# Attention and feed-forward on one core: v pieces as two transfers, early q and k turned in four quadrants, sums shared with GpSimd, and a new order

## The chip, the cores and the metric

The kernel runs on one core of a Trainium2 chip. The time is that of one execution on the device, in microseconds (us), and the median of several runs is compared. The core has five instruction streams: TensorE (PE, with its weight loads shown as PEld), VectorE (DVE), ScalarE (ACT), GpSimd (POOL) and SyncE (SP). SP issues every DMA of this kernel, one after the other, from one queue.

## The reference

```python
def _attn_ref(q, k, v):                 # 8 batches, 8 heads, 576 tokens, 64 per head
    q_d = q.reshape(B, H, Sd, factor, D).mean(axis=3)     # factor 4, Sd = 144; k_d and v_d alike
    out_d = sm_attn(q_d, k_d, v_d)                        # softmax attention over pooled tokens
    out_up = np.repeat(out_d, factor, axis=2)
    mask = np.abs(pos[:, None] - pos[None, :]) < factor   # local attention, 3 tokens each way
    ...
    return out_up + out_local

def _moe_ref(x, w_in, w_out, g_ln):     # x: 4608 tokens of 512, from all heads
    h = x @ w_in                        # 512 -> 1024
    sm = softmax(h)
    solu = h * sm
    ln = (solu - mean) / sqrt(var + 1e-06) * g_ln
    return ln @ w_out                   # 1024 -> 512
```

The weights come in as 64-bit floats and are turned into pairs of 32-bit values on the chip.

## The kernel before

**Tiles and stages.** Each of the 8 batches has 4 pairs of heads. Its q and k are brought into a layout with the head dimension on the partitions (tiles `qT`, `kT`), summed in groups of four tokens (`qd_flat`, `kd`, function `sums`), and used twice: class `Pooled` computes the pooled attention in two halves g (tiles `sd` for scores, `pd` for weights, `pdt`/`pdT` for their transposes, `po` for the output), and the classes `Local` and `PairOfLocals` the local attention in windows (tiles `sc`, `pl`, `plt`/`plT`, `xp`). Both add into `x`, one tile for each batch. `x` is cut into 36 tiles of 128 tokens for the feed-forward part: `xhl` splits such a tile into `xh` and `xl`, `ffn_in` multiplies by the first weights (`h`, line 813) and computes `e` and its statistics, `u` goes through DRAM to be transposed (`v<-u`), and `ffn_out` multiplies by the second weights (`o`, line 934). Four of the 36 span two batches; a tile needs all additions into the x of its batches.

**The early batches.** Batches 0 and 1 (`EARLY = 2`) are prepared by `EarlyBatch`: `load_one` brings one pair of q or k with plain rows, and `pair_steps` turns it on PE by small matmuls with the identity, 18 for q and then 18 for k, each kind in two quadrants of 64x64, followed by a copy out of PSUM. The later batches use many DMAs with short runs (line 257) and DVE's transposes (lines 445 and 449).

**The v pieces.** The pooled attention needs v summed by four tokens. `load_vs` brings one of three pieces `vs` of a batch: partitions 0 to 63 hold heads 0 to 3 and partitions 64 to 111 heads 4 to 7, for 48 groups of four tokens. For an early batch it issues four transfers (line 294), one for each pair of heads h and h + 4, each with a source of 2 heads x 64 rows x 1 KB. For a later batch it issues two (line 297), one of 64 partitions and one of 48, each with 4 heads x 1 KB for a partition. `pooled_vsum` (lines 466 and 469) adds each piece up into `vd`, which the `po` matmuls (line 795) read.

**The weights.** 16 pieces of 512 KB are loaded at the start (line 337); each takes four DVE operations (lines 348 to 361), of which one can go to GpSimd, and one subtraction.

**What sets the order.** The kernel makes a list of about 1800 steps (`plan`) and issues them in the order of the table `ORDER`, word for word; no scheduler moves anything afterwards. For steps in the table `OTHER`, `engine(usual, instead)` takes the second engine. So each engine's instructions, and SP's DMAs, stand in one fixed order, and an instruction that waits holds everything behind it on its engine. Buffers come from pools (six of `big` for the v pieces and weights, five of `vw` for the v windows of the local attention); a DMA into a buffer waits until its last reader is done.

**PE's idle time.** 24 steps (`keep_clock`, line 991) issue two matmuls each that compute nothing (`warm`), placed where PE would otherwise wait.

## Time and profile before

| | us |
|---|---|
| median of 3 runs | 638.21 (638.14 to 639.31) |
| the profiled execution | 636.78 |
| its span, first to last instruction | 635.0 |
| PE busy in the span | 569.0 (90%) |
| DVE, ACT, POOL busy | 455.6, 339.0, 282.8 |
| moved by DMA | 101.67 MB, 160 GB/s on average |

The span starts at the first instruction; places in it are given in us from there. A row of the chain of waits or of the timeline gives the start, the length, the engine, the line of the kernel, and the tile that is written, `<-`, the tiles that are read. SPq is time of SP's queue in issuing a DMA; a DMA row is the time from its issue until it landed. A row of the groups gives the busy time in all and the mean of one in ns, then the engine's idle time just before them and what ended it.

### The profile page before, as it was taken

What the parts mean: (1) busy time and instruction counts of PE and PEld (TensorE: products, weight loads), DVE (VectorE), ACT (ScalarE), POOL (GpSimd) and SP (SyncE); (2) the same over time, 40 slices, a digit from 0 to 9 for tenths busy, and PEclk for the clock granted to TensorE, in tenths of its full rate; (3) what the DMA queues carried; (4) which work ended last, traced back from release to release, by engine and by line L of the source; (5) the groups of instructions that cost most, each with busy time, mean ns of one, the idle gap of its engine ahead of it and who ended that gap; (6) DMA issues with size and microseconds to landing.
All of it is one profiled execution on the core that took longest, in us unless ns stands there. A gap on an engine that the chain in (4) does not pass through costs nothing.

```text
span 635.0 us, 17193 instructions
## 1 busy us (share of the span) xinstructions
PE 569.0 (90%) x6940; PEld 447.6 (70%) x6940; DVE 455.6 (72%) x673; ACT 339.0 (53%) x702; POOL 282.8 (45%) x365
## 2 busy tenths in 40 slices
PE   7863689951999999998999799899999999999997
PEld 4552567740777777777777677778887878778775
DVE  5953589942898977976986898477878688665451
ACT  4634567822468546754465447455653646453352
POOL 2540557821455945434284335724345444322211
PEclk9986789985899989999999899899999999999999
DMA  8344748723889868779786666755876384432341
GB/s 312 103 157 113 201 142 176 168 81 97 177 202 198 200 175 212 175 176 211 197 169 171 169 192 177 151 154 139 186 194 183 102 194 150 118 101 86 112 134 50
DMA packets 208255, 101.67 MB, mean 160 GB/s; under 512 B 163376, under 2 KB 192432, under 8 KB 208176
## 3 DMA queue, kind: packets, MB, share of 16 engines
q1 hardware_dynamic: 208176, 100.58, 60.6%
q8 instruction: 54, 0.88, 0.6%
q14 instruction: 25, 0.20, 0.1%
HBM read 67.51 MB, written 27.79 MB: 150 GB/s over the span
## 4 chain that ended last, share of the span: by engine, by line
PE 56%; SPq 15%; DMA 11%; DVE 9%; issue 3%; POOL 3%; ACT 3%; DVEq 0%; ACTq 0%; POOLq 0%
PE o L934 24%; PE h L813 20%; DMA vs<-in_v_dram 5%; SPq L257 4%; SPq L294 4%; SPq L886 2%; SPq L276 2%; PE po L795 2%; PE xp L696 2%; PE warm L991 2%; DMA v<-u 2%; PE sd L734 1%; PE pdt L776 1%; DMA qm<-in_q_dram 1%; SPq L270 1%
## 5 line engine op out<-in xcount | busy, mean ns | idle before, releaser
L934 PE MATMUL o<-wo_h,uh 128*128 128x512 f32 x288 | 119.2, 414 | 1.8 <-ACT osb L941 1.8
L813 PE MATMUL h<-wi_h,xh 128*128 128x512 f32 x288 | 116.4, 404 | 1.2 <-DVE e L827 1.2
L934 PE MATMUL o<-wo_l,uh 128*128 128x512 f32 x288 | 115.8, 402 | 0.0
L813 PE MATMUL h<-wi_l,xh 128*128 128x512 f32 x288 | 114.5, 398 | 0.0
L813 PE MATMUL h<-wi_h,xl 128*128 128x512 f32 x288 | 114.2, 397 | 0.0
L917 POOL TENSOR_TENSOR ul<-v,uh 128x512 fp32r<-128x512 f32 x39 | 51.5, 1321 | 79.1 <-ACT uh L914 67.7
L934 PE MATMUL o<-wo_h,ul 128*128 128x512 f32 x288 | 79.5, 398 | 0.9 <-DVE ul L917 0.8
L825 ACT ACTIVATE e<-h,st 128x1024 f32<-128x1024 f32 x36 | 40.1, 1115 | 63.7 <-DVE st L822 60.2
L934 PEld LDWEIGHTS o<-wo_h,uh 128*128 128x128 f32 x288 | 55.4, 192 | 17.5 <-ACT osb L941 2.6
L822 DVE TENSOR_REDUCE st<-h 128x1 f32<-128x1024 f32 x36 | 43.7, 1215 | 32.3 <-PE h L813 30.4
L907 DVE STREAM_TRANSPOSE v<-v 128x512 f32<-128x512 f32 x70 | 47.1, 691 | 27.2 <-DMA v<-u 27.2
L813 PEld LDWEIGHTS h<-wi_h,xh 128*128 128x128 f32 x288 | 54.5, 189 | 15.7 <-issue 1.4
L934 PEld LDWEIGHTS o<-wo_h,ul 128*128 128x128 f32 x288 | 54.1, 189 | 15.3 <-DVE ul L917 1.5
L813 PEld LDWEIGHTS h<-wi_h,xl 128*128 128x128 f32 x288 | 54.5, 189 | 14.0 <-DVE xl L968 0.7
L934 PEld LDWEIGHTS o<-wo_l,uh 128*128 128x128 f32 x288 | 55.4, 192 | 12.0
L813 PEld LDWEIGHTS h<-wi_l,xh 128*128 128x128 f32 x288 | 54.6, 189 | 12.3
L914 ACT ACTIVATE uh<-v 128x512 fp32r<-128x512 f32 x70 | 43.5, 624 | 34.6 <-DVE v L907 17.1
L831 POOL TENSOR_SCALAR st<-st 128x1 f32<-128x1 f32 x36 | 11.9, 331 | 101.0 <-DVE e L827 100.7
L827 DVE SCALAR_TENSOR_TENSOR e<-h,e 128x1024 f32<-128x1024 f32 x36 | 43.6, 1211 | 13.9 <-ACT e L825 13.6
L865 ACT ACTIVATE e<-e 128x1024 f32<-128x1024 f32 x35 | 36.8, 1052 | 17.2 <-DMA u<-e 17.2
L941 ACT ACTIVATE osb<-o,s 128x512 f32<-128x512 f32 x36 | 24.5, 680 | 36.1 <-PE o L934 15.1
L853 ACT ACTIVATE e<-e,st 128x1024 f32<-128x1024 f32 x27 | 30.9, 1145 | 14.1 <-POOL st L831 12.4
(124 smaller groups left out, 1087.1 us busy)
## 6 DMA issues: line engine op xcount, KB each, us to landing
u<-e SPq DMA_DIRECT2D x35, 512.0 KB
v<-u SPq DMA_DIRECT2D x140, 128.0 KB
out_dram<-osb SPq DMA_DIRECT2D x36, 256.0 KB
qm<-in_q_dram SPq DMA_DIRECT2D x96, 72.0 KB
km<-in_k_dram SPq DMA_DIRECT2D x96, 72.0 KB
vw<-in_v_dram SPq DMA_DIRECT2D x80, 64.0 KB
vw<-in_v_dram SPq DMA_DIRECT2D x40, 128.0 KB
plT<-pl SPq DMA_DIRECT2D x80, 64.0 KB
```

Source lines behind the costliest of these rows:

```text
L257: nc.sync.dma_start(t[nm][Q * 32:Q * 32 + 32, pr], src[b, 2 * pr + par, :, dh * 32:dh * 32 + 32].rearrange("(k t) d -> t k d", t=32),)
L294: nc.sync.dma_start(vs[:, h], source(h, [[H // 2 * S * D, 2], [FAC * D, 64]]))
L813: nc.tensor.matmul(hps[:, n, :], src[:, cc, :], wt[:, cc, n * 512:(n + 1) * 512], start=(cc == 0 and src is xh and wt is wi_h), stop=(cc = ...
L822: nc.vector.tensor_reduce(out=nmx, in_=hf, op=ALU.max, axis=AX.X, negate=True)
L825: nc.scalar.activation(e, hf, AF.Exp, bias=nmx, scale=1.0, accum_out=se)
L827: nc.vector.scalar_tensor_tensor(out=e, in0=hf, scalar=1.0, in1=e, op0=ALU.mult, op1=ALU.mult, accum_out=su)
L853: nc.scalar.activation(e, e, AF.Identity, bias=nmu, scale=1.0)
L865: nc.scalar.activation(e0, e, AF.Square, accum_out=m2)
L907: nc.vector.transpose(vg, vg)
L914: nc.scalar.activation(uh, tp, AF.Copy)
L917: (usual if v is None else engine(usual, nc.vector)).tensor_tensor(out=ul, in0=tp, in1=uh.bitcast(F32), op=ALU.subtract)
L934: nc.tensor.matmul(o, src[:, j, :], wt[:, 4 * g + j, :], start=(g == 0 and j == 0 and src is uh and wt is wo_h), stop=(g == 1 and j == 3 a ...
```

## The change

- `load_vs` uses for all batches the two transfers of 64 and 48 partitions that the later batches had.
- `EarlyBatch.pair_steps` turns q and k of a pair in one step, their 36 matmuls alternating; k is stored one head lower (`load_one` loads heads 2p+1 and 2p+2 together, and heads 0 and 7 alone), so that q uses two quadrants of PE and k the other two. The k tiles always come from the pool `ps_h`.
- `sums` may go to GpSimd, as three additions in place of one reduction.
- The pooled output that is not a batch's first is copied from PSUM into a part of the `pd` tile, and added into `x` from there, on GpSimd or on DVE.
- `ORDER` and `OTHER` are new tables: all steps are put in a new order, and OTHER has 157 entries in place of 103.

In the early part of SP's queue, behind the loads of batch 0, there stood (`vs_0` to `vs_2` are the three v pieces of batch 0, `qm` and `km` the q and k of batch 1, `vw` a v window, `stage` and `w_` weights):

```order
L294 DMA vs_0_369<-in_v_dram 128x1x256 x4
L486 DMA qm_364<-in_q_dram 128x576 x2
L486 DMA km_365<-in_k_dram 128x576
L337 DMA w_9_419<-in_moe_w_out_dram 128x1024
L486 DMA km_365<-in_k_dram 128x576
L294 DMA vs_1_422<-in_v_dram 128x1x256 x4
L337 DMA stage<-in_moe_w_in_dram 128x1024
L276 DMA vw_0_428<-in_v_dram 64x4x64 x4
L486 DMA km_365<-in_k_dram 128x576
L324 DMA g_sb<-in_moe_g_ln_dram 128x8x1
L294 DMA vs_2_436<-in_v_dram 128x1x256 x4
L486 DMA qm_364<-in_q_dram 128x576
```

And now at the same place of SP's queue:

```order
L494 DMA km_494<-in_k_dram 128x576 x2
L494 DMA qm_493<-in_q_dram 128x576
L494 DMA km_494<-in_k_dram 128x576
L494 DMA km_494<-in_k_dram 64x576
L293 DMA vs_1_500<-in_v_dram 64x4x256
L293 DMA vs_1_500<-in_v_dram 48x4x256
L280 DMA vw_1_503<-in_v_dram 64x4x64 x4
L336 DMA stage<-in_moe_w_in_dram 128x1024
L323 DMA g_sb<-in_moe_g_ln_dram 128x8x1
L293 DMA vs_2_511<-in_v_dram 64x4x256
L293 DMA vs_2_511<-in_v_dram 48x4x256
L494 DMA qm_493<-in_q_dram 128x576 x3
```

The last q of batch 1 stood behind three pieces of v in four transfers each; now it stands behind two pieces in two transfers each, and the third comes later.

Further on in SP's queue, before the pooled attention of batch 1 (`u` and `v` are the way of a feed-forward tile through DRAM, `qm` and `km` those of the next batch):

```order
L276 DMA vw_1_1656<-in_v_dram 64x4x64 x4
L294 DMA vs_2_1661<-in_v_dram 128x1x256 x4
L886 DMA v_1666<-u_1654 32x4x256 x4
L294 DMA vs_1_1671<-in_v_dram 128x1x256 x4
L863 DMA u_1955<-e_1579 128x1024
```

The same place in the new queue:

```order
L280 DMA vw_2_1545<-in_v_dram 64x4x64 x4
L280 DMA vw_4_1552<-in_v_dram 64x4x64 x4
L293 DMA vs_2_1557<-in_v_dram 64x4x256
L293 DMA vs_2_1557<-in_v_dram 48x4x256
L910 DMA v_1560<-u_1543 32x4x256 x4
L293 DMA vs_1_1565<-in_v_dram 64x4x256
L293 DMA vs_1_1565<-in_v_dram 48x4x256
```

The last two pieces of batch 1 still stand there one behind the other with a `v<-u` between them, now in four transfers in place of eight; another `vw` load stands ahead of them.

On DVE, the end of batch 1's pooled attention before (`x_1599` is the batch's x, `po_0` and `po_1` its two halves in PSUM):

```order
L466 TENSOR_TENSOR vs_1_1671<-vs_1_1671 112x4x128
L469 TENSOR_TENSOR vd_1368<-vs_1_1671 112x256
L907 STREAM_TRANSPOSE v_1666<-v_1666 128x4x128
L917 TENSOR_TENSOR ul_0_1951<-v_1666,uh_0_1950 128x512
L522 TENSOR_TENSOR x_1599<-x_1599,po_0_1981 128x2x576
L574 TENSOR_REDUCE mxl_0_1840<-pl_109 128x8
```

Now POOL has at this place (`pd_0_917` holds the copy of `po_0` that ACT makes; `qd_flat` is a group sum in three additions):

```order
L470 TENSOR_TENSOR vs_2_1557<-vs_2_1557 112x4x128
L473 TENSOR_TENSOR vd_1320<-vs_2_1557 112x256
L405 TENSOR_TENSOR qd_flat<-qT_1764 128x144
L405 TENSOR_TENSOR qd_flat<-qd_flat,qT_1764 128x144 x2
L823 TENSOR_TENSOR x_1647<-x_1647,pd_0_917 128x2x576
```

The first half's addition has moved from DVE, where it read PSUM, to POOL, where it reads the copy; the second half's is still on DVE. Over the whole program 8 of the 14 such additions are on DVE and 6 on POOL, and 25 of the 64 group sums are on POOL.

The diff, without the two tables:

```diff
 ORDER = """
-9 1 3 4 150 151 152 153 154 155 7 10 2 32 34 142 33 24 158 25 143 156 35 157 36 37 159 26 38 27
...
+147 148 149 8 5 150 151 4 13 2 155 156 157 152 158 159 160 153 34 27 33 139 41 17 6 35 40 26 25
...
@@ -284,20 +288,15 @@
 
     def load_vs(b, c):
         vs = big(f"vs_{b}_{c}").rearrange("p (h x) -> p h x", h=H // 2)
-
-        def source(head, dims):
-            at = v[b, head, c * KN * FAC, :]
-            return bass.AP(tensor=at.tensor, offset=at.offset, ap=[*dims, [1, FAC * D]])
-
-        if b < EARLY:
-            for h in range(H // 2):
-                nc.sync.dma_start(vs[:, h], source(h, [[H // 2 * S * D, 2], [FAC * D, 64]]))
-        else:
-            for half, n in ((0, 64), (1, KN)):
-                nc.sync.dma_start(
-                    vs[half * 64:half * 64 + n],
-                    source(half * (H // 2), [[FAC * D, n], [S * D, H // 2]]),
-                )
+        for half, n in ((0, 64), (1, KN)):
+            src = v[b, half * (H // 2), c * KN * FAC, :]
+            nc.sync.dma_start(
+                vs[half * 64:half * 64 + n],
+                bass.AP(
+                    tensor=src.tensor, offset=src.offset,
+                    ap=[[FAC * D, n], [S * D, H // 2], [1, FAC * D]],
+                ),
+            )
         return vs[0:ROOM]
 
 
@@ -398,9 +397,14 @@
 
 
     def sums(dst, src):
-        return nc.vector.tensor_reduce(
-            out=dst, in_=src.rearrange("x (s f) -> x s f", f=FAC), op=ALU.add, axis=AX.X
-        )
+        src = src.rearrange("x (s f) -> x s f", f=FAC)
+        if engine(nc.vector, nc.gpsimd) is nc.vector:
+            nc.vector.tensor_reduce(out=dst, in_=src, op=ALU.add, axis=AX.X)
+            return
+        for f in range(1, FAC):
+            nc.gpsimd.tensor_tensor(
+                out=dst, in0=dst if f > 1 else src[:, :, 0], in1=src[:, :, f], op=ALU.add
+            )
 
     class Batch:
 
@@ -482,32 +486,42 @@
                 for nm in ("q", "k")
             }
 
-        def load_one(self, pr, nm):
+        def load_one(self, head, nm):
+            src = {"q": q, "k": k}[nm][self.b]
+            lone = nm == "k" and head in (0, H - 1)
+            heads, at = ([head], 1 if head == 0 else 0) if lone else ([head, head + 1], 0)
+            slot = NPR - 1 if lone else head // 2
             nc.sync.dma_start(
-                self.qk[nm][:, pr * S:(pr + 1) * S],
-                {"q": q, "k": k}[nm][self.b, 2 * pr:2 * pr + 2].rearrange(
-                    "h (p t) d -> (h p) (t d)", t=self.TT
-                ),
+                self.qk[nm][at * 64:(at + len(heads)) * 64, slot * S:(slot + 1) * S],
+                src[heads[0]:heads[-1] + 1].rearrange("h (p t) d -> (h p) (t d)", t=self.TT),
             )
 
         def pair_steps(self, pr):
-            for nm, dst in (("q", self.qT[:, pr]), ("k", self.kT[:, pr])):
-                if self.b == 0 and nm == "k":
-                    tp = two_banks(ps_h, "h", f"kp_{pr}")
-                else:
-                    tp = two_banks(ps_a, "a", f"{nm}p_{self.b}_{pr}")
-                tp = tp.rearrange("p a n -> p (a n)")[:, 0:S].rearrange("p (t n) -> p t n", t=self.TT)
-                src = self.qk[nm][:, pr * S:(pr + 1) * S].rearrange("p (t d) -> p t d", t=self.TT)
-                for t in range(self.TT):
-                    for par in range(2):
-                        nc.tensor.matmul(
-                            tp[rows(par), t], src[rows(par), t], ident[rows(par), rows(par)],
-                            start=True, stop=True,
-                        )
-                yield
+            b, TT = self.b, self.TT
+            tq = two_banks(ps_a, "a", f"qp_{b}_{pr}")
+            tk = two_banks(ps_h, "h", f"kp_{b}_{pr}")
+            tq, tk = (
+                t.rearrange("p a n -> p (a n)")[:, 0:S].rearrange("p (t n) -> p t n", t=TT) for t in (tq, tk)
+            )
+            q_in, k_odd, k_even = (
+                self.qk[nm][:, slot * S:(slot + 1) * S].rearrange("p (t d) -> p t d", t=TT)
+                for nm, slot in (("q", pr), ("k", pr), ("k", (pr or NPR) - 1))
+            )
+            for t in range(TT):
+                for par in range(2):
+                    k_in, at = (k_odd, rows(0)) if par else (k_even, rows(1))
+                    nc.tensor.matmul(
+                        tq[rows(par), t], q_in[rows(par), t], ident[rows(par), rows(par)],
+                        start=True, stop=True,
+                    )
+                    nc.tensor.matmul(
+                        tk[rows(par), t], k_in[at, t], ident[at, at], start=True, stop=True,
+                    )
+            yield
+            for tp, dst in ((tq, self.qT[:, pr]), (tk, self.kT[:, pr])):
                 copy(
                     engine(nc.scalar, nc.vector),
-                    dst.rearrange("x (p t) -> x p t", t=self.TT), tp.rearrange("x t p -> x p t"),
+                    dst.rearrange("x (p t) -> x p t", t=TT), tp.rearrange("x t p -> x p t"),
                 )
                 yield
             sums(self.qd[pr], self.qT[:, pr])
@@ -798,7 +812,17 @@
                         )
             yield
             xv = bt.out()[:, g::2, :].rearrange("x r (s f) -> x r s f", f=FAC)
-            accumulate(xv, po.unsqueeze(3).broadcast_to([P, 2, SD, FAC]), self.first)
+            every = [P, 2, SD, FAC]
+            if self.first:
+                copy(engine(nc.scalar, nc.vector), xv, po.unsqueeze(3).broadcast_to(every))
+                yield
+                return
+            part = room[:, 0:2 * SD].rearrange("p (a n) -> p a n", a=2)
+            copy(engine(nc.scalar, nc.vector), part, po)
+            yield
+            engine(nc.gpsimd, nc.vector).tensor_tensor(
+                out=xv, in0=xv, in1=part.unsqueeze(3).broadcast_to(every), op=ALU.add
+            )
             yield
 
 
@@ -1008,13 +1032,17 @@
         row(ffn_out(i), 4)
 
     def prepare(bt):
+        if bt.b < EARLY:
+            for head in (H - 1, 0):
+                step(bt.load_one, head, "k")
         for pr in range(NPR):
             if bt.b < EARLY:
-                step(bt.load_one, pr, "q")
-                step(bt.load_one, pr, "k")
+                step(bt.load_one, 2 * pr, "q")
+                if pr < NPR - 1:
+                    step(bt.load_one, 2 * pr + 1, "k")
             else:
                 step(bt.load_q_k, pr)
-            row(bt.pair_steps(pr), 6 if bt.b < EARLY else 4)
+            row(bt.pair_steps(pr), 5 if bt.b < EARLY else 4)
 
     def values(bt):
         for c in range(KC):
@@ -1037,7 +1065,7 @@
                 continue
             if isinstance(it, Local):
                 step(bt.load_v, it.u)
-            row(it.steps(), 12 if isinstance(it, Pooled) else 11 if bt.b >= MASKED else 10)
+            row(it.steps(), 13 - late if isinstance(it, Pooled) else 11 if bt.b >= MASKED else 10)
 
     tiles = 0
     for n in range(WARM):
```

180 rows, old and new, of tables (ORDER, OTHER) are left out of this document.

## The prediction

> **What bounds the kernel now.** I read the page's slices first, then windows cut at the places where PE stops, then the chain of waits in the first 172 us, then the groups by form.
>
> ```profile
> PE 569.0 (90%) x6940; PEld 447.6 (70%) x6940; DVE 455.6 (72%) x673; ACT 339.0 (53%) x702; POOL 282.8 (45%) x365
> PE   7863689951999999998999799899999999999997
> DMA  8344748723889868779786666755876384432341
> ```
>
> PE is busy for 569.0 of 635.0 us, and the 66 us that are missing do not lie evenly: the third to sixth slice and the ninth and tenth (32 to 95 us and 127 to 159 us) hold nearly all of them, and there the DMA line is low too. From the eleventh slice on PE is full. So I cut windows at the two gaps. The columns are the length, then the busy time of PE, PEld, DVE, ACT and POOL, the granted PE clock, the DMA share and GB/s.
>
> ```profile
> 16.00:31.90 15.90, 13.23 (x274) 8.06 (x274) 15.52 (x26) 9.43 (x26) 8.48 (x7) 1.00 0.33 106
> 31.90:66.20 34.30, 14.93 (x358) 12.84 (x358) 14.53 (x25) 11.70 (x29) 8.31 (x8) 0.76 0.46 140
> 66.20:84.40 18.20, 15.39 (x357) 12.80 (x357) 11.45 (x19) 11.99 (x28) 10.13 (x11) 0.70 0.56 157
> 84.40:139.20 54.80, 49.56 (x812) 38.72 (x808) 47.54 (x79) 36.30 (x69) 37.63 (x37) 0.94 0.65 153
> 139.20:157.30 18.10, 0.79 (x12) 0.34 (x12) 2.49 (x5) 3.34 (x6) 1.99 (x2) 0.58 0.34 98
> 157.30:200.00 42.70, 42.70 (x370) 33.84 (x371) 36.72 (x56) 26.26 (x62) 20.99 (x30) 0.94 0.83 186
> 200.00:300.00 100.00, 95.85 (x1315) 75.54 (x1314) 80.70 (x116) 57.76 (x113) 54.00 (x69) 0.98 0.80 193
> 300.00:400.00 100.00, 95.16 (x1063) 74.94 (x1065) 82.78 (x118) 55.48 (x129) 49.92 (x63) 0.98 0.72 178
> 400.00:500.00 100.00, 97.97 (x1197) 78.80 (x1187) 77.06 (x109) 55.69 (x108) 44.47 (x63) 0.98 0.61 156
> 500.00:600.00 100.00, 99.87 (x874) 79.50 (x869) 65.41 (x87) 51.35 (x105) 37.58 (x57) 1.00 0.45 133
> ```
>
> Three regimes are to be seen. Where DVE gets its data it is the densest engine of the start: 15.52 of 15.90 us, and 47.54 of 54.80. Between 31.9 and 66.2 us every engine is under half busy, and between 139.2 and 157.3 us all of them stand. After 157.3 us PE is the bound; from 200 to 600 us it is idle for 11.15 us in all. So the start can be shortened, and what follows 157.3 us can hardly be. The chain tells who holds the two gaps (start, length, what).
>
> ```profile
> 39.35 11.12 DMA vs<-in_v_dram
> ...
> 53.66 3.69 SPq L294
> 57.40 8.70 DMA qm<-in_q_dram
> ...
> 66.23 2.08 PE qp L503 x34
> ...
> 142.01 3.36 SPq L294
> 145.41 10.46 DMA vs<-in_v_dram
> ...
> 157.27 1.28 PE po L795 x16
> ```
>
> Both gaps are the same thing: SP issuing the v pieces of the two early batches (line 294), and waiting or letting others wait for them. In the first, the last q transfer of batch 1 stands behind three v pieces in SP's queue and lands at 66.1 us; in the second, PE's po of batch 1 waits for a v piece itself.
>
> **The v pieces, term by term.** The same tensor is loaded in two forms in this trace.
>
> ```profile
> L297 SPq DMA_DIRECT2D vs<-in_v_dram x36: 598/607/865, 179.6 to 516.4; - x36
> L294 SPq DMA_DIRECT2D vs<-in_v_dram x24: 527/1520/3690, 20.1 to 145.4; - x24
> 262.03 6.44 DMA vs<-in_v_dram
> 290.25 4.70 DMA vs<-in_v_dram
> 50.50:57.40 6.90, 4.16 (x112) 3.74 (x112) 4.95 (x9) 4.87 (x18) 0.00 (x0) 0.54 0.15 44
> 179.00:190.00 11.00, 11.00 (x123) 8.80 (x122) 10.60 (x16) 5.95 (x10) 4.43 (x7) 1.00 0.89 214
> ```
>
> A piece of an early batch is four transfers of line 294, a piece of a later batch two of line 297. By medians the 24 issues cost SP 24 x 1.52 = 36.5 us, and in the new form the 12 will cost 12 x 0.607 = 7.3 us. The landing falls from the 10.46 and 11.12 us of the chain to 4.70 to 6.44 us. From 50.5 to 57.4 us, while line 294 was nearly all that SP issued, the DMA engines were busy for 0.15 of their time and moved 44 GB/s: 0.15 x 16 = 2.4 engines. From 179 to 190 us, with a piece of line 297 among the rest, the share was 0.89. So the old form is slow by its shape and not by a crowded moment: few engines carry it, and what is queued behind it waits for those few.
>
> Two rules of the Trainium skill, page "DMA: Bandwidth & Descriptors", bear on this. Its section "Rules for kernel authors" says that two transfers to disjoint halves of the partitions are not worth the trouble, because they serialize on the same engines, and that one of 128 partitions is better; by that the new pair would gain nothing, and the sum would stay at 0. Its section "Why a DMA increments its semaphore by 16 and not by 1" says that a transfer uses as many engines, up to 16, as divide the slowest dimension on both sides; the old source begins with a dimension of 2, the new ones with 64 and 48. The 0.15 beside the 0.89 agrees with the second.
>
> ```profile
> 84.38 0.50 PE L813 MATMUL h<-wi_h,xh 128*128 128x512 f32 x1
> ```
>
> *Up to the first feed-forward matmul.* In this profile the first h matmul starts at 84.4 us. The gap begins at 31.9 us, and from there to 84.4 us DVE has 14.53 + 11.45 = 25.98 us of work; by the two programs' orders the same work, give or take an instruction, stands ahead of that matmul after the change (92 and 93 DVE instructions in all). Packed as in the first window (15.52 / 15.90 = 0.98) it would take 26.6 us, packed as between 66.2 and 84.4 us (11.45 / 18.20 = 0.63) 41.3 us. I take the density of the next stage, 47.54 / 54.80 = 0.87, because that is what DVE reaches over a long stretch in which PE, DMA and DVE all work: 29.9 us. The first h matmul then starts at 61.8 us, **22.6 us earlier** (11.2 to 25.9).
>
> *From there to po of batch 1.* The stage takes 84.4 to 157.3 us, 72.9 us, of which the last 18.1 are the second gap. Its DVE work is 47.54 + 2.49 = 50.03 us; at 0.87 that is 57.5 us, at 0.98 51.1 us. The bad end: PE still waits there for a landing of 6.44 us and the two additions of a piece on POOL (1.31 + 0.78 us, below), 54.8 + 8.5 = 63.3 us. I take 57.5: **15.4 us earlier** (9.6 to 21.8).
>
> *The clock.* Behind the second gap PE runs at 0.94 for 42.7 us where it later has 0.98: 42.7 x 0.04 = **1.7 us**, gone with the gap.
>
> **The other edits.** They come with prices from the groups.
>
> ```profile
> L503 PE MATMUL kp<-ident,km 64*64 64x64 f32 x288 | 12.3, 247 | 12.6 <-DMA km<-in_k_dram 6.1 <-ACT qT L234 5.2 <-issue 1.3
> L551 PE MATMUL sc<-kT,qT 64*64 64x64 f32 x640 | 15.3, 241 | 0.2 <-ACT x L234 0.2
> L401 DVE TENSOR_REDUCE kd<-kT 128x144 f32<-128x576 f32 x32 | 23.5, 740 | 0.3
> L466 POOL TENSOR_TENSOR vs<-vs 112x512 f32<-112x512 f32 x16 | 21.0, 1313 | 30.0 <-DMA vs<-in_v_dram 21.1 <-issue 8.7
> L469 POOL TENSOR_TENSOR vd<-vs 112x256 f32<-112x256 f32 x16 | 12.5, 779 | 5.0 <-PE po L795 3.9
> L831 POOL TENSOR_SCALAR st<-st 128x1 f32<-128x1 f32 x36 | 11.9, 331 | 101.0 <-DVE e L827 100.7
> L522 DVE TENSOR_TENSOR x<-x,po 128x1152 f32<-128x1152 f32 x14 | 18.9, 1349 | 10.5 <-PE po L795 10.4
> L674 POOL TENSOR_TENSOR pl<-pl,mxl 128x1024 f32<-128x1024 f32 x8 | 16.8, 2103 | 10.8 <-DVE mxl L672 10.8
> L662 DVE TENSOR_TENSOR pl<-pl,mxl 128x1024 f32<-128x1024 f32 x3 | 3.6, 1213 | 0.0
> ```
>
> *Quadrants.* The matmuls of the early transposes stay as many; two quadrants become four. Busy per record is 12.3 / 288 = 43 ns now, and 15.3 / 640 = 24 ns where four quadrants already run (sc), so each k or q of a pair could lose up to 36 x 19 ns = 0.7 us, 16 of them 11 us of PE time. I book **0**: it falls before 84.4 us, where DVE sets the pace, and it is covered by that. Were DVE not the cover, half of it at most would show, 5 us. The price on the other side: a pair's k now needs two transfers, and PE's first pair needs three transfers instead of two, one transfer (288 KB) more at 106 to 214 GB/s, 1.3 to 2.8 us, once, at the start, where PE does warm-up matmuls until then. I book 0 there as well.
>
> *Group sums.* By the order 25 of the 64 sums go to POOL, as three additions each. DVE loses 25 x 0.74 = 18.5 us. An addition of 144 elements lies between the 0.33 us of a one-element operation and the 0.78 us of 256 elements; 75 of them are 25 to 58 us more on POOL, which has 352 us idle. Four of the 25 stand ahead of po of batch 1, 3 us of DVE's 76, so the start gains next to nothing from them; later PE is the bound, and less DVE work buys at most the idle time of PE. **0**, within -5 and +3 us.
>
> *Pooled addition.* The 14 additions that are not a batch's first become a copy out of PSUM and an addition, 8 on DVE and 6 on POOL. An addition is 1.35 us now; on POOL 1152 elements take about 2.4 us (2.10 x 1152 / 1024), on DVE 1.36 (1.213 x 1152 / 1024), and the copy of 288 elements 0.34 by the same scale (1.35 x 288 / 1152). Behind it wait xh, xl and the h matmuls of the first tile of that batch, so each adds 0.4 to 1.5 us to a chain beside which PE has o and h of earlier tiles: PE idles 11.15 us in all from 200 to 600 us, where most of them lie. **0**, up to +8 us if half of them show.
>
> **The sum.** 22.6 + 15.4 + 1.7 = 39.7 us. The profiled execution took 636.78 us (span 635.0 and 1.78 around it), so the changed kernel's would take 597.1 us. The median of the runs, 638.21 us, lies 1.43 us above the profiled one; the same offset gives **598.5 us**. The good ends (25.9 + 21.8 + 1.7 + 5) give 583.8 us, the bad ones (11.2 + 9.6 + 1.0 - 8) 624.4 us, both on the median's scale.
>
> **Rivals.**
>
> *The transfers become the bound of the start.* From 31.9 to 84.4 us the DMA engines worked 0.46 x 34.3 + 0.56 x 18.2 = 26.0 us. To have moved all that by 61.8 us they would need a share of 0.87, which the trace shows (0.89) but only later. At the 0.65 of the long stage it takes 40 us, and the first h matmul comes at 71.9 us, 12.5 us earlier; with the second stage at its bad end, 9.6, and 1 us of clock that is 23.1 us: 613.7 and 1.4, **615 us**. For it: SP's queue is in order, and the batch 1 pieces stand behind a vw load that waits for a buffer. Against: 12 issues of 0.6 us instead of 24 of 1.5 leave the queue gaps that it never had.
>
> *The new form is no faster here.* If the two transfers of a piece take turns on the same few engines, each piece holds its queue as before (10.46 and 11.12 us), both gaps stay, and the time is that of before, **638 us**. The 4.70 and 6.44 us speak against it, though they come from stages with other neighbours. The skill's rule against two halves, above, is this case.
>
> *Slower: the pooled addition on the path.* If the copy, a 2.4 us addition on POOL, and a queue ahead of it there delay the first h tile of every batch, the excess over the old addition (0.34 + 2.4 - 1.35 = 1.4 us) and 0.8 us of queue come to 2.2 us for each of the 14. With only half of the two gaps closed (19 us) and 14 x 2.2 = 31 us lost, the time is 638.2 - 19 + 31 = **650 us**. It decides once each costs more than 19 / 14 = 1.4 us. Against it: PE had work in hand at nearly every such place.
>
> The skill's page "SBUF — State Buffer", section "Who interferes with whom", adds to this rival: a DVE instruction with two inputs in SBUF contends with a GpSimd instruction that reads SBUF, and one of them stops until the other ends. The old addition read one input from PSUM, the new one reads both from SBUF; by the rule up to a POOL instruction's length (2.10 us) could come on top of each of the 8 on DVE. This trace shows no addition of that shape, so the extra is an estimate.
>
> **How the numbers follow.** The forecast has a chance of 0.66 (584 to 610 us), the transfers as bound 0.20 (610 to 627), no gain 0.05, slower by the pooled addition 0.05, and better than the good ends 0.04. The range from 584 to 622 us leaves out the last three and the upper edge of the second, under 2 in 10. Within 0.2% is about what a measurement of this kernel can tell from no change. Faster by more: 0.66 + 0.20 + 0.04 and a little of the no-gain case, 0.91; within it 0.03; slower 0.06.
>
> **What would show it.** In the changed profile the first h matmul should start near 62 us, the PE slices of 32 to 64 us should hold eights instead of 6 and 3, and the ninth and tenth slice should be full. No v piece of batches 0 and 1 should be on the chain with more than 7 us. SP should issue such a transfer in 0.6 to 0.9 us. DVE should be over 0.85 busy from 20 us to po of batch 1. After that place PE's time should be the 477.7 us it is now, within 8 us. I am wrong if DVE is under 0.75 busy there with waits on DMA (first rival), or if PE's idle time from 200 us on grows by more than 8 us with x or xh as releaser (third).

## The result, and the profile after

The changed kernel takes **608.7 us** (median of four runs, 608.27 to 610.92) where the kernel before takes 638.17 us beside it (637.59 to 639.31): a ratio of 0.9543, with a 95% interval from 0.9517 to 0.957. The forecast was 598.5 us, the range 584 to 622. So about 29.5 us of the 39.7 that were forecast came, and 10 did not.

The page of the changed kernel, in the lines that were shown of before:

```profile
PE 561.8 (92%) x6940; PEld 436.8 (72%) x6940; DVE 462.7 (76%) x661; ACT 332.3 (55%) x702; POOL 336.0 (55%) x441
PE   6777978999989899897999799899999999999997
DMA  8698677785888877768768768564466726223321
```

Both gaps are gone: the slices that held 6, 3, 6, 8 and 5, 1 hold 7s and 9s. But the third and fourth slice hold 7s, not the eights that were forecast. The line of the v pieces in the changed kernel (ns of an issue, least, median and most; first and last start):

```profile
L293 SPq DMA_DIRECT2D vs<-in_v_dram x48: 595/609/1694, 26.6 to 474.8; - x48
...
DMA to landing us min/median/max: 3.6/4.3/9.2
```

The matmuls of h from 50 us on, in the same columns:

```profile
L837 PE MATMUL h<-wi_h,xh x23: 392/394/632, 67.8 to 99.5; 128*128 128x512 f32 x23
```

And those of po from 105 us on, which are batch 1's:

```profile
L809 PE MATMUL po<-pdT,vd x32: 282/283/334, 122.7 to 127.0; 48*64 48x144 f32 x32
```

All v pieces are now of one form, 0.609 us of SP by the median of all 48 issues. For the 12 issues of batches 0 and 1 alone it is 0.612 us, and these landed after 6.1 us by the median, 9.2 us at most. The first h matmul starts at 67.8 us (84.4 before, 61.8 forecast), po of batch 1 at 122.7 (157.3 before). Windows cut at these two places, and one from 200 to 400 us (length, busy time of PE, PEld, DVE, ACT, POOL, granted clock, DMA share, GB/s):

```profile
20.00:67.80 47.80, 37.86 (x977) 25.86 (x977) 39.22 (x64) 31.50 (x81) 30.25 (x25) 0.83 0.77 197
67.80:122.70 54.90, 48.25 (x811) 37.29 (x806) 53.52 (x82) 37.39 (x73) 40.10 (x44) 0.97 0.74 165
122.70:609.00 486.30, 464.39 (x4936) 368.24 (x4936) 357.45 (x490) 255.95 (x539) 259.93 (x358) 0.98 0.61 158
200.00:400.00 200.00, 184.66 (x2252) 146.06 (x2251) 155.54 (x211) 106.48 (x233) 125.12 (x166) 0.97 0.75 183
```

The second stage takes 54.9 us, 2.6 us less than was taken for it. Time is missing at two places. The first stage ends 6 us late. And from po of batch 1 to the end it now takes 486.3 us where it took 635.0 - 157.27 = 477.7: 8.6 us that were won ahead are lost again behind. These places are read from one execution of each kernel: the changed kernel's took 610.92 us, 2.2 us above its median, and the old one's 636.78 us, 1.4 us below, so by the profiles 3.6 us more are missing than by the medians. PE is idle for 15.3 us between 200 and 400 us, before for 8.99 (4.15 + 4.84). The experiments had to answer two questions: is the transfer's form really the whole gain, and what takes the 6 and the 8.6 us?

### The profile page after: what moved, and what is told of

It reads as the page before. It is cut to its first block, busy times and chain, and to the rows that moved or that the text cites. A ratio compares the mean times of both kernels' runs of the same rounds, so it can differ in the third digit from the quotient of the medians.

```text
span 609.0 us, 17190 instructions
## 1 busy us (share of the span) xinstructions
PE 561.8 (92%) x6940; PEld 436.8 (72%) x6940; DVE 462.7 (76%) x661; ACT 332.3 (55%) x702; POOL 336.0 (55%) x441
## 4 chain that ended last, share of the span: by engine, by line
PE 54%; DVE 16%; DMA 10%; SPq 9%; issue 5%; POOL 3%; ACT 3%; DVEq 0%; ACTq 0%; POOLq 0%
PE o L958 23%; PE h L837 22%; SPq L261 3%; DMA km<-in_k_dram 2%; DMA qm<-in_q_dram 2%; SPq L910 2%; SPq L698 2%; DMA u<-e 2%; DVE e L851 1%; DVE st L846 1%; PE xp L710 1%; PE po L809 1%; DVE w L356 1%; PE sc L652 1%; PE pdt L790 1%
## 5 line engine op out<-in xcount | busy, mean ns | idle before, releaser
L837 PE MATMUL h<-wi_h,xh 128*128 128x512 f32 x288 | 119.5, 415 | 3.2 <-DVE e L851 3.2
L837 PE MATMUL h<-wi_h,xl 128*128 128x512 f32 x288 | 117.6, 408 | 3.2 <-DVE xl L992 2.1
L958 PE MATMUL o<-wo_h,uh 128*128 128x512 f32 x288 | 117.7, 409 | 2.3 <-ACT osb L965 2.3
L837 PE MATMUL h<-wi_l,xh 128*128 128x512 f32 x288 | 116.9, 406 | 0.0
L958 PE MATMUL o<-wo_l,uh 128*128 128x512 f32 x288 | 114.3, 397 | 0.0
L837 PEld LDWEIGHTS h<-wi_h,xl 128*128 128x128 f32 x288 | 56.3, 196 | 18.4 <-DVE xl L992 3.2
L837 PEld LDWEIGHTS h<-wi_h,xh 128*128 128x128 f32 x288 | 56.1, 195 | 18.3 <-issue 3.6
L837 PEld LDWEIGHTS h<-wi_l,xh 128*128 128x128 f32 x288 | 56.3, 196 | 12.7
L941 POOL TENSOR_TENSOR ul<-v,uh 128x512 fp32r<-128x512 f32 x29 | 38.2, 1320 | 30.2 <-ACT uh L938 21.0
L992 POOL TENSOR_TENSOR xl<-x,xh 128x512 fp32r<-128x512 f32 (+1 forms) x26 | 31.1, 1201 | 30.8 <-ACT xh L989 30.5
```

The costliest lines, as they stand in the source:

```text
L837: nc.tensor.matmul(hps[:, n, :], src[:, cc, :], wt[:, cc, n * 512:(n + 1) * 512], start=(cc == 0 and src is xh and wt is wi_h), stop=(cc = ...
L941: (usual if v is None else engine(usual, nc.vector)).tensor_tensor(out=ul, in0=tp, in1=uh.bitcast(F32), op=ALU.subtract)
L958: nc.tensor.matmul(o, src[:, j, :], wt[:, 4 * g + j, :], start=(g == 0 and j == 0 and src is uh and wt is wo_h), stop=(g == 1 and j == 3 a ...
L992: engine(nc.gpsimd, nc.vector).tensor_tensor(out=l, in0=src, in1=h.bitcast(F32), op=ALU.subtract)
```

## The experiments

Each was timed in turns with the kernel before; a ratio with its interval is to that kernel on the same chip.

### The form of the transfers alone, and taken back

The first run is the kernel before, its order untouched, with one edit:

```diff
-        if b < EARLY:
-            for h in range(H // 2):
-                nc.sync.dma_start(vs[:, h], source(h, [[H // 2 * S * D, 2], [FAC * D, 64]]))
-        else:
-            for half, n in ((0, 64), (1, KN)):
+        for half, n in ((0, 64), (1, KN)):
...
```

> The kernel before, with its own order, and only the v pieces of the two early batches loaded as two transfers of 64 and 48 partitions. Theory (the shape of these transfers makes both gaps): the first h matmul comes at 62 to 72 us instead of 84.4, the ninth and tenth slice fill, and the time is 600 to 615 us, a ratio of 0.94 to 0.965. Rival (the gain of the change comes from its new order and its other edits): the gaps mostly stay and the time is over 625 us, ratio above 0.98.

Measured: **596.17 us**, ratio 0.9338 (0.9306 to 0.937), that is 12.5 us less than the changed kernel. Its slices, its first h matmuls, and its windows cut at them and at po of batch 1:

```profile
PE   7887899999898999899979999999999999999996
```

```profile
L809 PE MATMUL h<-wi_h,xh x28: 392/396/776, 61.8 to 99.7; 128*128 128x512 f32 x28
```

```profile
20.00:61.80 41.80, 34.77 (x894) 25.30 (x894) 36.84 (x63) 29.94 (x78) 25.76 (x22) 0.96 0.90 226
61.80:114.50 52.70, 48.35 (x815) 37.33 (x808) 51.97 (x84) 38.59 (x73) 39.74 (x39) 0.97 0.79 178
114.50:593.00 478.50, 459.99 (x4937) 364.99 (x4936) 354.15 (x501) 260.61 (x538) 211.52 (x292) 0.99 0.63 162
200.00:400.00 200.00, 192.16 (x2363) 152.43 (x2362) 157.84 (x225) 114.24 (x241) 95.62 (x125) 0.99 0.72 177
```

Here the first h matmul starts at 61.8 us, DVE is 36.84 / 41.80 = 0.88 busy up to it, and behind po of batch 1 the time is 478.5 us, as before. This is the kernel that the prediction worked out; the one that was timed had other things in it.

The opposite: the changed kernel with the old four transfers for the early batches.

```diff
+        if b < EARLY:
+            for h in range(H // 2):
...
+                        ap=[[H // 2 * S * D, 2], [FAC * D, 64], [1, FAC * D]],
...
+            return vs[0:ROOM]
```

> The changed kernel with the v pieces of the two early batches again as four transfers of two heads each; everything else, the order too, as changed. Theory: both gaps come back, SP needs over 1.3 us for each of the 24 issues, and the time is 630 to 650 us, ratio 0.99 to 1.02. Rival (the new order places the pieces so that their shape does not matter): 608 to 616 us, ratio below 0.965.

Measured: 650.28 us, ratio 1.0179 (1.0148 to 1.021). Its slices and its row of the old form:

```profile
PE   6743688592999998998999989979999999999997
```

```profile
L294 SPq DMA_DIRECT2D vs<-in_v_dram x24: 520/1596/4384, 26.5 to 151.0; - x24
```

The gaps are back, the first at the same slices (4, 3, 6, 8), the second in the tenth (2), with 5 in the eighth. The form carries the gain in either order, and without it the rest of the change is slower than the kernel before by 11.2 us (650.28 against 639.07 beside it).

### The shape, or the number of transfers?

The new form differs in two ways: two transfers instead of four, and partitions as the slowest dimension instead of the 2. (It also moves less: 256 and 192 KB for a piece instead of four times 128 KB, since the second half stops at 48 partitions.) In the kernel before, four transfers per piece again, but each by partitions:

```diff
-            for h in range(H // 2):
-                nc.sync.dma_start(vs[:, h], source(h, [[H // 2 * S * D, 2], [FAC * D, 64]]))
+            for half, n in ((0, 64), (1, KN)):
+                for h in range(0, H // 2, 2):
+                    nc.sync.dma_start(
+                        vs[half * 64:half * 64 + n, h:h + 2],
+                        source(half * (H // 2) + h, [[FAC * D, n], [S * D, 2]]),
+                    )
```

> The kernel before, with a v piece of the early batches still in four transfers, each now of two heads over 64 or 48 partitions, the partitions being the slowest dimension of source and tile (before: four transfers of one head and its counterpart over 64 rows each, the 2 being the slowest dimension). It tells the shape from the number of transfers. Theory (the shape is what costs): SP needs 0.5 to 0.8 us for each of the 24 issues, first h matmul at 61 to 65 us, 595 to 601 us. Rival (four transfers instead of two are what costs): issues of over 1.2 us, the gaps stay in part, 612 to 630 us.

Its line of the early v pieces, and its first h matmuls:

```profile
L295 SPq DMA_DIRECT2D vs<-in_v_dram x24: 428/597/873, 19.7 to 109.9; - x24
```

```profile
L817 PE MATMUL h<-wi_h,xh x28: 388/394/775, 61.4 to 99.3; 128*128 128x512 f32 x28
```

Measured: **595.78 us**, ratio 0.9335 (0.9268 to 0.9402), the same as with two. Twenty-four issues that cost 1.52 us each cost 0.597 us in this shape. So the number of transfers costs nothing here, and the shape is the cause. Both new forms also move an eighth fewer bytes; no run changes that alone, but an eighth is far from the factor of 2.5 between the issues.

### The first stage: how q and k are loaded

The changed kernel with q and k of a pair loaded whole and turned one after the other in two quadrants; order, sums and additions as changed:

```diff
-            lone = nm == "k" and head in (0, H - 1)
...
+            if nm == "k" and head == H - 1:
+                return
+            pr = (head + 1) // 2
...
+            for nm, tp in (("q", tq), ("k", tk)):
...
```

> The changed kernel with the transposes of the early batches in two quadrants again: q and k of a pair each loaded by one transfer, k not shifted, first the 18 matmuls of q and then the 18 of k. Theory of the prediction (quadrants are worth nothing, DVE sets the pace): the time of the changed kernel within 2 us, 607 to 611 us. Rival one (the three transfers that a pair then needs delay the start, which was 6 us later than predicted): 602 to 606 us, and the first h matmul 3 to 6 us ahead of 67.8. Rival two (four quadrants save PE time that shows): 612 to 617 us.

Measured: 604.72 us, ratio 0.9472 (0.9439 to 0.9505); in a second run, as the base of an experiment below, 606.67 us, 0.9498 (0.9459 to 0.9538). That is 2 to 4 us better than the changed kernel: the first interval lies clear of the changed kernel's (0.9517 to 0.957), the second overlaps it. The first h matmul starts at 62.7 us in the first run's profile and at 65.5 us in the second's. This run lacks both the shifted loads and the alternating matmuls, so a third kernel keeps the shifted loads and only turns all of q ahead of all of k:

```diff
             for t in range(TT):
                 for par in range(2):
-                    k_in, at = (k_odd, rows(0)) if par else (k_even, rows(1))
                     nc.tensor.matmul(
                         tq[rows(par), t], q_in[rows(par), t], ident[rows(par), rows(par)],
...
+            for t in range(TT):
+                for par in range(2):
+                    k_in, at = (k_odd, rows(0)) if par else (k_even, rows(1))
                     nc.tensor.matmul(
```

> The changed kernel with its loads (k shifted by a head, the two lone halves) but the 36 matmuls of q ahead of the 36 of k instead of alternating; the run with two quadrants was 4 us faster than the changed kernel and had neither the loads nor the alternation. Theory (the loads are what costs: the lone halves of 64 partitions keep the DMA engines busy until 20 us and the last pairs wait): no gain, 607 to 611 us, and PE still stands some 3 us between 13 and 21 us. Rival (the alternation on four quadrants costs): 603 to 606 us.

Measured: 608.04 us, ratio 0.9561 (0.9518 to 0.9605), the time of the changed kernel, with the first h matmul at 65.8 us. So the 2 to 4 us go with the loads, not with the alternation. Three views of the changed kernel: windows from 12 to 20 us, the landing of k up to 24 us (count, KB, median us), and PE's timeline around 20 us with the idle time in brackets:

```profile
12.00:16.00 4.00, 3.20 (x122) 2.31 (x126) 3.90 (x8) 1.71 (x3) 0.58 (x2) 1.00 1.05 291
16.00:20.00 4.00, 0.46 (x28) 0.32 (x18) 0.78 (x2) 1.18 (x2) 2.28 (x3) 0.90 0.97 309
```

```profile
km<-in_k_dram SPq DMA_DIRECT2D x3, 288.0 KB, 7.7
km<-in_k_dram SPq DMA_DIRECT2D x2, 144.0 KB, 8.9
```

```profile
20.07 0.36 PE L513 MATMUL qp<-ident,qm 64*64 64x64 f32 x1 [3.61 <-issue]
```

The first two of the kernel with two quadrants and whole loads:

```profile
12.00:16.00 4.00, 3.94 (x102) 3.05 (x99) 3.26 (x6) 2.65 (x5) 0.47 (x2) 1.00 1.05 422
16.00:20.00 4.00, 3.63 (x100) 3.00 (x100) 4.00 (x6) 2.49 (x4) 2.70 (x3) 1.00 0.53 209
```

```profile
km<-in_k_dram SPq DMA_DIRECT2D x8, 288.0 KB, 5.7
```

With the lone halves of 64 partitions the DMA engines are as busy (1.05) but move 291 instead of 422 GB/s from 12 to 16 us (287 with shifted loads and no alternation, 401 in the kernel before with the new form alone), half a k takes longer (8.9 us) than a whole one, and the engines are full until 20 us where otherwise they are half done by then. PE meanwhile stands for 3.61 us in the middle of a pair, "issue": nothing that the profile shows is waited for. With whole loads PE stands for 0.37 us at that place, with shifted loads and no alternation 2.44; over all kernels in the new order it is 0.23 to 1.19 us in the four with whole loads and 2.28 to 3.71 us in the four with the halves. SP, whose next k load (line 494) needs the buffer that these transposes free, goes on at 24.30 us instead of 21.55. What PE stands for is not shown; that the stall is longer where the lone halves are loaded is. Full DMA engines are not its condition: the kernel before stands for 1.33 us in the same stretch, at a DMA share of 0.02.

How the stall reaches the h matmul can be read from DVE. In the changed kernel DVE stands for ACT's copy of the q that PE was turning:

```profile
21.48 0.75 DVE L402 TENSOR_REDUCE qd_flat<-qT 128x144 f32<-128x576 f32 x1 [3.99 <-ACT qT L238]
```

So less of its work is done by 24 us, and what is left over stands ahead of the first h matmul. The profiles of the new order with the new form, and the form alone beside them ("again" is the second run with two quadrants):

| kernel | order | loads of k | DVE busy, 16 to 24 us | first h matmul |
|---|---|---|---|---|
| form alone | old | whole | 7.94 | 61.8 |
| two quadrants | new | whole | 7.93 | 62.7 |
| two quadrants, again | new | whole | 5.96 | 65.5 |
| 8 additions from PSUM (below) | new | whole | 7.71 | 62.3 |
| all on DVE (below) | new | whole | 6.65 | 64.1 |
| shifted loads, no alternation | new | halves | 4.88 | 65.8 |
| all sums on DVE (below) | new | halves | 3.35 | 65.3 |
| changed kernel | new | halves | 3.27 | 67.8 |

The halves go with less work of DVE by 24 us and with a later matmul. But two executions of one kernel lie 2.8 us apart, so a part only of the 6 us can be put down to the loads.

### The other edits, one by one

All 64 group sums on DVE in the changed kernel:

```diff
-        if engine(nc.vector, nc.gpsimd) is nc.vector:
+        if True:
```

> The changed kernel with all 64 group sums on DVE again, one reduction each; everything else as changed. Theory of the prediction (the 25 sums on POOL bring and cost nothing): 606.5 to 611 us. Rival one (POOL, fuller by these sums, is what lost 8 us behind the start): 602 to 606 us, with less idle time of PE between 200 and 400 us. Rival two (DVE needed the relief): 612 to 618 us.

Measured: 609.08 us, ratio 0.9527 (0.9506 to 0.9549): nothing, as predicted.

The addition in two steps, in the order of before and with the new form of the v pieces, so that 596.2 us is the base (edit for POOL; for DVE the last line reads nc.vector):

```diff
-            accumulate(xv, po.unsqueeze(3).broadcast_to([P, 2, SD, FAC]), self.first)
...
+                copy(nc.scalar, part, po)
+                nc.gpsimd.tensor_tensor(
...
```

> The kernel before with the new form of the v pieces (596.2 us) and each of the 14 later pooled additions as a copy on ACT and an addition on POOL right behind it, in the order of before. Theory one (the addition on POOL is what costs): the 14 cost 0.4 to 1.5 us each, 602 to 616 us. Theory two (PE has other work there): 595 to 598.5 us.

> As the run before, with the 14 additions on DVE behind their copies on ACT. Theory one (only POOL's length costs): 595 to 598 us. Rival (a DVE addition with both inputs in SBUF stops for POOL's instructions, or the longer chain of copy and addition shows): 599 to 606 us, and single additions of over 2 us.

Measured: on POOL **616.9 us**, ratio 0.9698 (0.964 to 0.9755); on DVE **602.36 us**, ratio 0.9455 (0.9412 to 0.9498). Against the medians of the base, from another set of runs, the 14 cost 20.7 us on POOL, 1.5 each, and 6.2 us on DVE, 0.4 each. The additions' own rows, what their engine waited for ahead of them and who waited for them, on POOL and then on DVE:

```profile
L803 POOL TENSOR_TENSOR x<-x,pd x14: 2218/2257/2467, 116.2 to 535.6; 128x1152 f32<-128x1152 f32 x14
...
its engine sat idle before it (us, times) until:
  ACT pd L234: 16.4, 6
...
who waited for it (us, times):
  ACT xh L969: 17.6, 5
```

```profile
L803 DVE TENSOR_TENSOR x<-x,pd x14: 1294/1358/1696, 116.5 to 521.6; 128x1152 f32<-128x1152 f32 x14
...
its engine sat idle before it (us, times) until:
  ACT pd L234: 11.9, 7
who waited for it (us, times):
  ACT xh L969: 7.0, 5
```

And the additions from PSUM with the form alone:

```profile
L518 DVE TENSOR_TENSOR x<-x,po x14: 1304/1349/1355, 115.7 to 516.8; 128x1152 f32<-128x1152 f32 x14
```

By the medians the addition is hardly longer on DVE than from PSUM (1.358 us, 1.349 there), and 0.9 us longer on POOL. With the form alone DVE stood for po for 9.3 us ahead of the 14, and ACT's xh, which begins the next tile, stood for them for 8.6 us. On POOL xh stands for 17.6 us, so there the price is seen on the way to the next tile. On DVE the engine stands for ACT's copy for 11.9 us and xh for 7.0; where the 6.2 us are lost is not shown by these rows.

### The order

One kernel keeps the new tables but has the operations of the run just above: two quadrants, whole loads, all sums and all additions on DVE, copies apart. It and that run, timed side by side, differ in the tables, with which go the engine of some copies, and in where batch 1's k is turned (PSUM of h instead of a).

> The changed kernel with two quadrants and whole loads, all group sums on DVE and all 14 later pooled additions on DVE (still a copy and an addition from SBUF); what is left of the change is the form of the v pieces, the order and the copies. Theory one (the six additions on POOL, 2.3 us each, and POOL's other new work lost the 8 us behind the start): 595 to 600 us, and PE idles under 10 us from 200 to 400 us. Theory two (the new order lost them): 602 to 607 us, and PE idles 13 to 17 us there as it did with two quadrants (16.0).

Measured: 609.77 us, ratio 0.9554 (0.9515 to 0.9593), against 602.36 and 0.9455 (0.9412 to 0.9498) in the order of before. The windows of the new tables' kernel, then of the old tables' one:

```profile
119.70:609.10 489.40, 465.88 (x4936) 369.00 (x4936) 373.28 (x517) 255.32 (x539) 206.78 (x288) 0.98 0.62 157
200.00:400.00 200.00, 187.29 (x2254) 148.54 (x2255) 163.11 (x228) 105.12 (x232) 92.68 (x125) 0.95 0.76 183
```

```profile
114.90:598.70 483.80, 462.72 (x4937) 365.75 (x4936) 357.36 (x501) 264.81 (x552) 218.19 (x292) 0.99 0.63 160
200.00:400.00 200.00, 191.02 (x2352) 151.13 (x2351) 156.44 (x221) 113.60 (x240) 95.19 (x124) 0.98 0.72 175
```

The new tables cost 7.4 us with these operations. By the two profiled executions 4.8 us lie ahead of po of batch 1 (119.7 for 114.9) and 5.6 behind (489.4 for 483.8), together 3 us more than by the medians, as the one is the slowest of its four and the other the fastest; from 200 to 400 us PE idles 12.7 us instead of 9.0, at a clock of 0.95 instead of 0.98. The tables were made for 25 sums and six additions on POOL: with those left there the same loads took 604.72 and 606.67 us, so the 7.4 us are the price of the new order for operations that it was not made for. The tables were not tried with the operations of before, whose steps they don't number.

Last, 8 of the 14 additions back to one DVE instruction from PSUM, with the new tables, two quadrants and whole loads:

```diff
+            if (b, g) in ((1, 0), (1, 1), (2, 1), (3, 0), (3, 1), (5, 1), (6, 0), (7, 1)):
+                nc.vector.tensor_tensor(
+                    out=xv, in0=xv, in1=po.unsqueeze(3).broadcast_to(every), op=ALU.add
+                )
...
```

> The changed kernel with two quadrants and whole loads, and 8 of the 14 later pooled additions as one DVE addition from PSUM again, at the place of the copy (the other 6 stand ahead of the batch's local part in the new order, and stay copy and addition). Theory one (copy and addition in two steps lost the 8 us behind the start): 8 of 14 come back, 4 to 6 us under the same kernel without this edit, 598 to 601 us. Theory two (the new order lost them): within 2 us of the kernel without this edit, 602.5 to 607 us.

> The kernel with two quadrants and whole loads once more, beside the run before it: 603 to 607 us under both theories, the base for that run.

Measured: 611.3 us, ratio 0.9585 (0.955 to 0.9621), beside 606.67 us and 0.9498 (0.9459 to 0.9538) for its base. Undoing the edit made it slower by 4.6 us, the opposite of what theory one wanted, and more than the 2 us of theory two. So the two steps are not a tax that can be taken back within the new order: there the DVE addition stands where a short copy was meant to stand, though that this is the reason is not shown. In the old order the two steps cost 6 us, in the new one they are better kept. The stretch behind po of batch 1 is as long with all sums on DVE (486.5 us) and with whole loads (485.2 and 486.6 us) as in the changed kernel (486.3 us), so neither is what lengthens it. So the 8.6 us belong to the new tables and the two steps together; how they divide is not settled, since the tables fit the two steps and can't be run without them as they are.

### A version that beats both, and a try to better it

The kernel before with the new form alone, in two or in four transfers, is faster than both kernels: 596.17 and 595.78 us. In it DVE fills the stage up to po of batch 1, so four sums of k of batch 2 that stand there were put on POOL, three additions each:

```diff
+            if self.b == 2:
...
+                    nc.gpsimd.tensor_tensor(
...
```

> The kernel before with the new form of the v pieces, and the four group sums of k of batch 2 as three additions each on POOL. In the run with the form alone DVE was busy 51.97 of the 52.70 us up to po of batch 1, and these four sums stand there, 3.0 us of it. Theory (DVE bounds that stage, POOL has room): 593 to 596 us. Rival (the twelve additions of 0.57 us hold up POOL's subtractions and halves of softmax, or the 3 us are lost again behind): 596 to 599 us.

Measured: 599.48 us, ratio 0.9408 (0.9368 to 0.9449). No gain, 3.3 us more by medians, with intervals that just overlap. The trace shows where it is lost: from the first h matmul to po of batch 1 it takes 57.0 us instead of 52.7, and there PE waits once for a softmax product `pl` on POOL (3.0 us) and DVE once for a weight operation on POOL (4.1 us), as neither did with the form alone. Behind po it takes 477.7 us, as before. So it is the rival of this run that the trace bears out.

## Why the prediction was right, and where it was not

**The gaps and their cause: right, and shown.** The 24 transfers made both gaps; taking them out of the old kernel closes both, putting them into the new one opens both. An issue of an early piece came to 0.612 us (0.607 forecast) and landed after 6.1 us by the median (4.70 to 6.44 forecast). One took 9.2 us, but no landing of a v piece is on the chain.

Of the two rules of the Trainium skill, page "DMA: Bandwidth & Descriptors", the runs bear out one. The section "Why a DMA increments its semaphore by 16 and not by 1" agrees with the run that kept four transfers and put the partitions in the slowest dimension (595.78 us). The rule in the section "Rules for kernel authors", by which two halves are not worth the trouble, does not decide this case: here the other choice was not one transfer of 128 partitions but four whose slowest dimension was 2.

**Term 1, the first h matmul at 61.8 us: right for the form, 6 us too early for the whole change.** With the form alone it is 61.8 us, and from 31.9 us on, where the forecast counts, DVE has 25.51 us of work at a density of 0.85 (25.98 and 0.87 taken). That the place agrees to 0.1 us is partly luck, as the two differences cancel. In the changed kernel it is 67.8: the density is 0.84, as good, but 29.98 us of work stand there, for DVE had done less by then. The step that failed is the 0 booked for the quadrants and their loads, with its reason that DVE covers what PE loses ahead of the h matmul: the loads were priced as one more transfer of 1.3 to 2.8 us, behind warm-up matmuls. The runs show a lower rate beside the halves (291 for 422 GB/s), PE's stall of 3.61 us, SP's restart 2.75 us later, and DVE waiting for what PE turns instead of covering it (3.27 us busy from 16 to 24 us instead of 7.94). With whole loads the h matmul comes at 62.3 to 65.5 us in four profiles, so the rest of the 6 us, of which no run shows the cause, is the order's or differs between executions.

**Term 2, 57.5 us from there to po of batch 1: right, somewhat long.** 54.9 us, and 52.7 with the form alone: DVE ran at 0.975 and 0.986, near the 0.98 that was kept as the good end.

**The clock, 1.7 us: right at its place, not in sum.** Behind po of batch 1, where it was 0.94, the granted clock is now 1.00. But from 160 to 200 us it is lower, and over all that follows po it is 0.98, as it was before; with the form alone it is 0.99. In six other profiles of the new order with the new form it is 1.00 from 160 to 200 us; why it is 0.91 here is not shown.

```profile
122.70:160.00 37.30, 37.27 (x326) 28.93 (x327) 36.07 (x57) 25.44 (x63) 23.36 (x35) 1.00 0.70 157
160.00:200.00 40.00, 37.81 (x610) 29.98 (x609) 33.02 (x41) 20.20 (x33) 30.52 (x35) 0.91 0.83 183
```

**Group sums 0: right**, 609.08 beside 608.7 us.

**Pooled addition 0, up to 8 us, and "after po of batch 1 unchanged within 8 us": here the prediction failed by its own test, narrowly**, with 8.6 us. Four more profiles of the new order, with six additions on POOL as here, have 485.1 to 486.6 us there, 7.4 to 8.9 more than before. The reason given was that PE had work in hand at nearly every such place. That was read from the trace of the old order, and the new order is another one: its stretch from 200 to 400 us idles 12.7 us even with the additions on DVE. The prediction gave no term to the new tables behind po of batch 1. In the old order the reason fails too: the 14 cost 6.2 us on DVE and 20.7 on POOL, 0.4 and 1.5 us each, the whole of the 0.4 to 1.5 us that were worked out for an addition, so in the old order little of them was hidden.

**The rivals.** The transfers as bound of the start (615 us): the result lies between it and the forecast. DVE's share from 20 us to po of batch 1, the sign that was named, is (39.22 + 53.52) / (47.80 + 54.90) = 0.90, above the 0.85 that the forecast wanted; up to the first h matmul alone it is 0.82. With the form alone the transfers reached the share that this rival doubted, 0.90 up to 61.8 us, so the new v pieces leave them room to carry the start. The new form no faster: refuted. Slower by the pooled addition: its price, 1.5 us each on POOL, is real, and is what the old order would have paid; the changed kernel has six there, and PE's idle time from 200 to 600 us grew by 4.7 us (15.88 for 11.15), not 8, and over the whole stretch behind po of batch 1 by 7.0 (21.9 for 14.9).

**The contention: there, and smaller than its bound.** In the changed kernel one of DVE's eight additions from SBUF is long, and so are two of POOL's six beside DVE's:

```profile
L823 DVE TENSOR_TENSOR x<-x,pd x8: 1352/1370/2239, 129.4 to 533.1; 128x1152 f32<-128x1152 f32 x8
L823 POOL TENSOR_TENSOR x<-x,pd x6: 2239/2281/3397, 125.0 to 395.0; 128x1152 f32<-128x1152 f32 x6
```

The long one starts at 193.05 us, while POOL has 1.02 us left of a product (line 688), and takes 0.87 us more than the median. POOL's own addition starts beside it at 194.03 us, when DVE has 1.26 us left, and takes 1.10 us more. In the old order an addition that starts with 0.48 us left of a POOL operation takes 0.35 us more. The additions from PSUM with the form alone, of which several begin inside such POOL operations too, stay at 1.304 to 1.355 us. So the one that comes later stands for about the rest of the other, and only where the two meet; the prediction's bound was a whole POOL instruction for each. The Trainium skill's page "SBUF — State Buffer", section "Who interferes with whom", says that a DVE instruction with two inputs in SBUF contends with a GpSimd instruction that reads SBUF. These traces agree with it.

## What to carry to other kernels

Make the partitions the slowest dimension of a transfer on both sides: where the slowest dimension was 2, nearly the same bytes (512 for 448 KB a piece), in as many transfers, held their queue 2.5 times as long here (1.52 for 0.597 us), and everything behind them. When a change brings a new order along with its edits, price the order as a term of its own, and time the one edit that carries the gain in the old order: here that was 12.5 us faster than the whole. An addition out of PSUM that is split into a copy and an addition can cost time even where the addition itself is no longer than before: 6.2 us for 14 of them on DVE. And before a difference of 2 or 3 us is read out of one profile, take a second one of the same kernel: here the first h matmul moved by 2.8 us.

## What was not expected of the hardware

A load in two halves of 64 partitions, among whole ones, went with a lower rate at the same busy share of the DMA engines: 281 to 291 GB/s in the four kernels that have them, 420 to 422 in the four of the same order that don't. PE can stand for 3.61 us in the middle of a run of equal matmuls with nothing to wait for in the profile. And an addition on DVE with both inputs in SBUF, begun while POOL works, is longer by about what POOL has left (0.87 for 1.02 us), where one with an input in PSUM is not.
